# Rounded routing features, negations on ScalarE, a subtraction on GpSimd, and the spacing of zero writes in a three-stage kernel

## The chip, the core and the metric

The kernel runs on one core of one Trainium2 chip. The metric is the device time of one execution in microseconds; lower is better. TensorE (PE in the profile) multiplies, VectorE (DVE), ScalarE (ACT) and GpSimd (POOL) work on tiles, and SP issues most DMAs. Each engine takes its own instructions strictly in the order in which the build put them, and waits on semaphores for the others.

## What is computed

Three stages are chained. The input `x` is 4 batches of 3072 tokens of 256 numbers.

```python
# 1: spectral layer, per batch
X  = np.fft.rfft(x, axis=1)
Yr = X.real @ w_r - X.imag @ w_i + b_r
Yi = X.real @ w_i + X.imag @ w_r + b_i
Y  = sign(Y) * maximum(abs(Y) - 0.01, 0)       # real and imaginary part each
x  = np.fft.irfft(Y, n=3072, axis=1).reshape(12288, 256)
# 2: mixture of 8 experts, top 1, 384 places each, filled in token order
e  = argmax(x @ w_gate);  gate = softmax(...)[e]
h  = maximum(disp @ w1, 0);  y = h @ w2;  out[i] = gate[i] * y[e, place[i]]
# 3: dense layer
h  = x @ w_in;  out = (h * sigmoid(h)) @ w_out
```

Tokens that find no place give zero rows. With these inputs the experts are full early in batch 1, so the kernel works on batch 0 and a third of what follows, and a branch (never taken here) holds the rest.

## The kernel before

**Products.** Nearly all products run as three rounded passes (`mm3`, lines 208 to 210): each operand is split into a rounded high part and a rounded low part (`split`, lines 192 and 200), and high*high, low*high and high*low are summed in PSUM. Rounded tiles have the type FR (float32r), all others F32.

**Spectral stage.** `s1` makes the first half of the transform and stores it in DRAM (`a_d`). `kphase` then walks over 24 frequencies, two a step (k = 0, 2 to 22, 12 steps). `forward` makes the spectrum `xp` in PSUM (L418) and from it the tile `xk` with four parts: high (ACT, L432), low (DVE, L433), minus high (ACT, L434) and minus low (DVE, L435). `shrink` multiplies by the weights into `yp`, adds the bias (DVE, `y`, L456; the tile `y` has one buffer), clamps (DVE, L458) and subtracts the clamped part (DVE, L459), which gives `cl`. `back` (L465, `bp`) multiplies `cl` of three steps earlier by the inverse table; ACT copies `bp` to `bo` and after every second step issues its write to `b_d`. The steps of batch 0 are mixed with `s1` of batch 1 and with the rounding of `w_in`; those of batch 1 are mixed with `is2` of batch 0, which ends the inverse transform and computes the gate.

**Routing.** `route` counts places and builds `ft`, two features for each of 24 slots-by-expert columns (the token's number and its gate weight), and `pm`, a one-hot matrix for each group of 128 tokens. `tb = pm.T @ ft` (L723) is 24 F32 products for batch 0 and 8 for batch 1, each of which the chip runs as two passes. The sum goes to `table`, `slots` reads source rows and gate weights from it, `gather` fetches the rows with indirect DMAs on GpSimd (L978), DVE scales them (L982), PE transposes them (`gtp`, L990) and ACT and DVE split them into `xT`, which the first expert's product `hp` needs.

**Experts.** `experts` runs a first and a second phase per expert in the order first 0, 1, 2, second 0, 1, 2, first 3, 4, second 3, 4 and so on. Expert weights stream through four staging buffers (`st`, L966). Beside the first phases runs `third`, which reads `b_d` of batch 1 (`br`, L546) and makes the rows of its first third (`ps`, L549). Rows of the output that no token fills are written as zeros (`zero_out`, L217, 48 DMAs of 256 KB on SP). The finished rows go out by indirect DMAs on GpSimd (L1072).

A timeline planner in the build sets each engine's order from its own estimates, so that an edit also moves instructions that it doesn't name.

Of the kernel before, what the change touches and what calls it, by code (L numbers as in the profile page):

```python
# [9 lines left out]
F32 = mybir.dt.float32  # L10
FR = mybir.dt.float32r
I32 = mybir.dt.int32
ALU = mybir.AluOpType
AF = mybir.ActivationFunctionType
# [7 lines left out]
E, F, CAP = 8, 1024, 384  # L22
DFF = 2048
P = 128
# [4 lines left out]
NEAR = S + QB * TW  # L29
SC = CAP // P  # L30
NS = E * CAP
NF = 2
STEP = 4096
ROUND = 1.5 * 2.0 ** 30
MID = 0.5 * (P - 1)
# [107 lines left out]
def raw(t):  # L143
    return t.bitcast(F32)
# [18 lines left out]
class Kernel:  # L163
# [239 lines left out]
    def kphase(self, b, ads, ahead=False):  # L403

        nc, kp = self.nc, self.kp
        v = nc.vector
        a_d = ads[b]
        b_d = self.bds[b] = self.dr.tile([NK, P, D], F32, name=f"b_d{b}")
        KG = 4

        def fetch(k):
            ar = kp.tile([P, KG, D], F32, tag="ar", name="ar")
            self.fetched = nc.sync.dma_start(out=ar, in_=a_d[k:k + KG].rearrange("k p c -> p k c")).ins
            return ar

        def spectrum(xp, ar, kq, tb):

            return [nc.tensor.matmul(xp[:, c], ar[:, kq, c * P:(c + 1) * P], c2[:, tb], start=True, stop=True).ins for c in range(2)]  # L418

        def forward(k, ar):  # L420
            first = k == 0
            kq = k % KG
            xk = kp.tile([P, 2, 4, 192], FR, tag="xk", name="xk", bufs=3)
            xp = self.pk.tile([P, 4, P], F32, tag="xp", name="xp", bufs=self.xb)
            behind = self.gated[PACE[k // 2]] if b == 1 and k // 2 in PACE else None
            for j in range(2):
                for ins in spectrum(xp[:, 2 * j:2 * j + 2], ar, kq + j, k + j + 1):
                    if behind:
                        self.after(ins, behind)
            js = slice(2, 4) if first else slice(0, 4)  # L430
            up, mid, low = slice(64, 192), slice(128, 192), slice(0, 64)
            nc.scalar.copy(xk[:, 0, :, up], xp)  # L432
            v.tensor_tensor(xk[:, 1, :, up], xp, raw(xk[:, 0, :, up]), ALU.subtract)  # L433
            nc.scalar.activation(xk[:, 0, js, low], xp[:, js, 64:], AF.Copy, scale=-1.0)  # L434
            v.tensor_tensor(xk[:, 1, js, low], raw(xk[:, 0, js, mid]), xp[:, js, 64:], ALU.subtract)  # L435
            xo = None
            if first:
                xp = self.pk.tile([P, 4, P], F32, tag="xp", name="xp", bufs=self.xb)
                spectrum(xp, ar, 0, 0)
                xo = kp.tile([P, 2, 2, P], FR, name="xo", bufs=1)  # L440
                self.split("av", xo[:, 0], xo[:, 1], xp[:, :2])
            return xk, xo

        def shrink(k, xk, xo):
            yp = self.pk.tile([P, 2, D], F32, tag="yq" if k % 4 and (b != 1 or k > 12) else "yp", name="yp", bufs=1)
            for j in range(2):
                for jj in range(2):
                    for c in range(2):
                        if jj and xo is not None and not j:
                            l = [xo[:, h, c] for h in range(2)]  # L450
                        else:
                            l = [xk[:, h, 2 * j + c, 64 - 64 * jj:192 - 64 * jj] for h in range(2)]
                        self.mm3(yp[:, j], l[0], l[1], wri[:, jj, 0, c], wri[:, jj, 1, c], jj + c == 0, jj + c == 2)
            y = kp.tile([P, 2, D], F32, tag="y", name="y", bufs=1)
            bias = self.bias if xo is not None else self.bias[:, 1:2].to_broadcast([P, 2, D])
            v.tensor_tensor(y, yp, bias, ALU.add)  # L456
            cl = kp.tile([P, 2, D], F32, tag="cl", name="cl", bufs=3)
            v.tensor_scalar(cl, y, LAM, -LAM, ALU.min, ALU.max)  # L458
            self.shrunk = v.tensor_tensor(cl, y, cl, ALU.subtract).ins  # L459
            return cl  # L460

        def back(k, bo, cl):
            bp = self.pk.tile([P, 2, D], F32, tag="bp", name="bp", bufs=1)
            for j in range(2):
                self.backed = nc.tensor.matmul(bp[:, j], c3[:, k + j], cl[:, j], start=True, stop=True).ins  # L465
            self.hi("a", bo[:, k % KG:k % KG + 2], bp)
            if k % KG + 2 == KG:
                nc.scalar.dma_start(out=b_d[k + 2 - KG:k + 2].rearrange("k p c -> p k c"), in_=bo)

        x, y = {}, {}  # L470
        ars = [fetch(0), fetch(KG)] if ahead else []
        if ahead:
            yield
        c2, c3, wri = self.c2, self.c3, self.wri
        for k in range(0, NK + 6, 2):
            if k < NK:
                if k % KG == 0:
                    ar = ars.pop(0) if ars else fetch(k)
                x[k] = forward(k, ar)
            if 2 <= k < NK + 2:  # L480
                y[k - 2] = shrink(k - 2, *x.pop(k - 2))
            if k >= 6:
                if (k - 6) % KG == 0:
                    bo = kp.tile([P, KG, D], F32, tag="bo", name="bo")
                back(k - 6, bo, y.pop(k - 6))
            yield
# [168 lines left out]
    def route(self, b, qbs, res):  # L655

        nc, bp, ps, rt = self.nc, self.bp, self.ps, self.rt
        v = nc.vector
        oh, m2, sm = res[b]
        NB = len(qbs)  # L660
        NC = NB * GT
# [17 lines left out]
        nc.gpsimd.tensor_scalar(sm, sm, 1e-9, None, ALU.add)  # L679
        gt = bp.tile([P, NC, 1], F32, tag="gt", name="gt", bufs=1)  # L680
        v.reciprocal(gt, sm.rearrange("p b g o -> p (b g) o"))
        base = bp.tile([P, E, NB, 1], F32, tag="base", name="base", bufs=1)
        v.scalar_tensor_tensor(base[:, :, :, 0], bs[:, 0], -1.0, self.carry.to_broadcast([P, E, NB]), ALU.add, ALU.add)
        v.tensor_tensor(inc, base.to_broadcast([P, E, NB, GT]), oh, ALU.mult)
# [7 lines left out]
        r = bp.tile([P, NC, 1], F32, tag="r", name="r", bufs=1)  # L692
        v.scalar_tensor_tensor(r, blk, -ROUND, pos, ALU.add, ALU.subtract)
        sh = [P, NC, SC * E]
        ft = bp.tile([P, NC, NF, SC * E], F32, tag="ft", name="ft", bufs=1)
        mk = ft[:, :, 1]
        tok = rt[:, 2 * P + qbs[0] * GT:2 * P + qbs[0] * GT + NC].rearrange("p (c o) -> p c o", o=1)
        v.tensor_tensor(mk, blk.to_broadcast(sh), self.col.to_broadcast(sh), ALU.is_equal)
        v.tensor_tensor(ft[:, :, 0], mk, tok.to_broadcast(sh), ALU.mult)
        prev = v.tensor_tensor(mk, mk, gt.to_broadcast(sh), ALU.mult)  # L700
        tb = ps.tile([P, NF, SC * E], F32, tag="ps", name="tb")
        sh = [P, GT, P]
        for j in range(NB):
            pm = bp.tile(sh, F32, tag="xt", name="pm", bufs=self.sb)
            how = "v" if b else PMS[j]
            if how == "a":
                for t in range(GT):
                    nc.scalar.activation(pm[:, t], self.iota, AF.Abs, scale=-1.0, bias=r[:, j * GT + t])
                nc.scalar.activation(pm, pm, AF.Relu, scale=-1.0, bias=1.0)
            elif how == "v":  # L710
                here = v.tensor_tensor(pm, self.iota.rearrange("p (o m) -> p o m", o=1).to_broadcast(sh),
                                       r[:, j * GT:(j + 1) * GT].to_broadcast(sh), ALU.is_equal)
                self.after(here.ins, prev.ins)
                self.made = here.ins
            else:
                for t in range(GT):
                    e = v if how == "s" else nc.gpsimd
                    here = e.tensor_scalar(pm[:, t], self.iota, r[:, j * GT + t], None, ALU.is_equal)
                    if how == "s":
                        self.after(here.ins, prev.ins)  # L720
                        self.made = here.ins
            for t in range(GT):
                nc.tensor.matmul(tb, pm[:, t], ft[:, j * GT + t], start=(j + t == 0), stop=(j * GT + t == NC - 1))  # L723
# [35 lines left out]
    def slots(self, pool, s0, s1, sel, tag):  # L759

        v = self.nc.vector
# [14 lines left out]
        v.tensor_scalar(a, ent[:, :, 0:SC], -1.0, 0.0, ALU.add, ALU.max)  # L776
        v.tensor_copy(src, a)
        gw = pool.tile(w, F32, name=f"gw{tag}", bufs=1)
        v.tensor_copy(gw, ent[:, :, SC:2 * SC])
        b = pool.tile(w, F32, name=f"slb{tag}", bufs=1)  # L780
        dst = pool.tile(w, I32, name=f"dst{tag}", bufs=1)
        v.tensor_scalar(b, ent[:, :, 0:SC], 0.5, BIG, ALU.is_lt, ALU.mult)
# [88 lines left out]
    def experts(self, again=False):  # L871
# [44 lines left out]
        n = 0  # L916
        for at, ph in enumerate(order):
# [11 lines left out]
            for m, _ in enumerate(part):  # L929
                n += 1  # L930
                while due is not None and due <= n:
                    due = next(side, None)
                if n in AHEAD or (ph == E and m % 2 == 0):
                    next(fw, None)
                if ph >= E:
                    for _ in range(2 if ph == E else n % 2):
                        self.zero_out()
                if m == last - 2 and after < E:
                    xs[after] = self.turn(xg.pop(after))
# [179 lines left out]
```

## Time and profile before

| | |
|---|---|
| median of 3 runs | 649.71 us (649.0 to 649.79) |
| profiled execution: time, span | 650.9 us, 649.1 us |
| PE busy | 618.7 us (95%) |
| DVE, ACT, POOL busy | 320.3 us (49%), 305.8 us (47%), 75.5 us (12%) |
| granted TensorE clock, mean | 0.975 of full speed |

Busy time of PE is modelled, and a busy PE may be a slow one: at half of the granted clock a pass takes twice as long and still counts as busy. So the table by stretches is read with its column of the granted clock (PEclk), and the pitch of passes (start to start) is read from the timeline.

### The profile page before, as it was taken

How to read it: one execution, taken by the hardware profiler on the slowest of the kernel's cores; microseconds unless marked ns; L12 is line 12 of the kernel's file. 1: busy time of each engine (PE TensorE's matmuls, PEld its weight loads, DVE VectorE, ACT ScalarE, POOL GpSimd, SP SyncE). 2: the span in 40 equal slices, each digit the busy share in tenths (PEclk: the TensorE clock that was granted, in tenths of full speed). 3: DMA queues.
4: the chain of work that ended last, by engine and by line, in shares of the span. 5: the costliest groups of instructions: out<-in, count | busy, mean ns of one | idle time of the engine just before them, and what ended most of it. 6: DMA issues, size and time to landing. Idle time of an engine off the chain costs nothing. (4 is left out here: it accounts for less than half of the span.)

```text
span 649.1 us, 10932 instructions
## 1 busy us (share of the span) xinstructions
PE 618.7 (95%) x4108; PEld 567.7 (87%) x4108; DVE 320.3 (49%) x655; ACT 305.8 (47%) x624; POOL 75.5 (12%) x86
## 2 busy tenths in 40 slices
PE   7689999999998999999999999999999999999993
PEld 3367889767997679999999999999999999999993
DVE  3349986455966467886222246522236632223330
ACT  4434543343433445466544445545445554544450
POOL 1002220000023001062101032000121000101001
PEclk7899999999977999999999999999999999999998
DMA  8996945983337776599700025300004300000000
GB/s 251 294 264 210 303 153 174 200 258 96 130 123 219 215 203 218 167 310 330 246 1 26 1 71 149 110 5 10 16 21 127 119 13 2 25 1 25 1 2 29
DMA packets 64085, 83.03 MB, mean 128 GB/s; under 512 B 5588, under 2 KB 53688, under 8 KB 64024
## 3 DMA queue, kind: packets, MB, share of 16 engines
q1 hardware_dynamic: 52056, 66.52, 33.9%
q10 hardware_dynamic: 9664, 9.44, 4.9%
q0 software_dynamic: 2304, 6.29, 3.0%
q8 instruction: 34, 0.56, 0.3%
q14 instruction: 27, 0.22, 0.1%
HBM read 49.73 MB, written 32.51 MB: 127 GB/s over the span
## 5 line engine op out<-in xcount | busy, mean ns | idle before, releaser
L200 DVE TENSOR_TENSOR gl<-sg,gh 128x384 fp32r<-128x384 f32 x118 | 67.1, 574 | 160.6 <-ACT gh L192 154.7
L1042 ACT ACTIVATE sg<-h 128x384 f32<-128x384 f32 x128 | 62.4, 491 | 108.6 <-PE h L210 103.8
L209 PE MATMUL o<-wo,gl 128*128 128x256 f32 x354 | 93.2, 282 | 0.5 <-DVE gl L200 0.5
L210 PE MATMUL o<-wo,gh 128*128 128x256 f32 x354 | 93.1, 282 | 0.0
L208 PE MATMUL h<-yT,wi 128*128 128x384 f32 x256 | 86.3, 337 | 0.4 <-ACT yT L192 0.4
L209 PE MATMUL h<-yT,wi 128*128 128x384 f32 x256 | 86.1, 336 | 0.0
L210 PE MATMUL h<-yT,wi 128*128 128x384 f32 x256 | 85.7, 337 | 0.0
L208 PE MATMUL o<-wo,gh 128*128 128x256 f32 x354 | 74.6, 282 | 0.0
L209 PEld LDWEIGHTS o<-wo,gl 128*128 128x128 f32 x354 | 67.1, 190 | 0.9 <-DVE gl L200 0.7
L210 PEld LDWEIGHTS o<-wo,gh 128*128 128x128 f32 x354 | 67.2, 190 | 0.0
L192 ACT CAST gh<-sg 128x384 fp32r<-128x384 f32 x118 | 59.9, 514 | 6.9 <-PE o L210 4.0
L208 PEld LDWEIGHTS o<-wo,gh 128*128 128x128 f32 x354 | 60.3, 189 | 0.0
L208 PE MATMUL yp<-wri,xk 128*128 128x256 f32 x188 | 56.3, 299 | 0.1
L209 PE MATMUL yp<-wri,xk 128*128 128x256 f32 x188 | 55.0, 293 | 0.3 <-DVE xk L435 0.3
L210 PE MATMUL yp<-wri,xk 128*128 128x256 f32 x188 | 54.0, 287 | 0.0
L200 DVE TENSOR_TENSOR w<-st,w 128x512 fp32r<-128x512 f32 x64 | 44.4, 696 | 17.3 <-ACT w L192 17.2
L192 ACT CAST w<-st 128x512 fp32r<-128x512 f32 x64 | 39.3, 620 | 28.3 <-PE hp L210 14.8
L1008 ACT ACTIVATE hh<-hp 128x384 fp32r<-128x384 f32 x64 | 31.3, 491 | 41.6 <-PE hp L210 18.6
L208 PEld LDWEIGHTS h<-yT,wi 128*128 128x128 f32 x256 | 48.2, 188 | 0.7 <-ACT yT L192 0.7
L1009 DVE SCALAR_TENSOR_TENSOR hl<-hp,hh 128x384 fp32r<-128x384 f32 x64 | 35.0, 553 | 27.3 <-ACT hh L1008 24.9
L209 PEld LDWEIGHTS h<-yT,wi 128*128 128x128 f32 x256 | 48.1, 188 | 0.0
L210 PEld LDWEIGHTS h<-yT,wi 128*128 128x128 f32 x256 | 48.1, 188 | 0.0
(213 smaller groups left out, 1214.4 us busy)
## 6 DMA issues: line engine op xcount, KB each, us to landing
st<-in_moe_w SPq DMA_DIRECT2D x64, 256.0 KB
out<-zt SPq DMA_DIRECT2D x48, 256.0 KB
a_d<-ao SPq DMA_DIRECT2D x16, 384.0 KB
ar<-a_d SPq DMA_DIRECT2D x12, 512.0 KB
b_d<-bo ACTq DMA_DIRECT2D x12, 512.0 KB
xt<-in_x SPq DMA_DIRECT2D x15, 384.0 KB
nt<-in_moe_w_in SPq DMA_DIRECT2D x8, 512.0 KB
nt<-in_moe_w_out SPq DMA_DIRECT2D x16, 256.0 KB
```

Of the source, the lines that this page charges most:

```text
L192: self.nc.scalar.copy(dst, src)
L200: return e.tensor_tensor(dst, src, raw(hi), ALU.subtract).ins
L208: first = nc.tensor.matmul(out, lh, rh, start=start, stop=False)
L209: nc.tensor.matmul(out, ll, rh, start=False, stop=False)
L210: return first.ins, nc.tensor.matmul(out, lh, rl, start=False, stop=stop).ins
L1008: nc.scalar.activation(hh, hp, AF.Relu)
L1009: self.evicted = nc.vector.scalar_tensor_tensor(hl, hp, 0.0, raw(hh), ALU.max, ALU.subtract).ins
L1042: nc.scalar.activation(sg, hp, AF.Silu)
```

## The change

Four edits. (1) The negated low part is made by ScalarE from the finished low part, not by VectorE from PSUM. (2) The routing product runs on rounded operands: the gate weight is split into a rounded high and low part, so there are three features and not two, `mk` gets a tile of its own, and `slots` adds the two parts. (3) The last subtraction of `shrink` runs on GpSimd in batch 1. (4) While the second phase of expert 0 runs, each of its steps issues one zero write and not two.

```diff
-NF = 2
+NF = 3
@@ forward
-            v.tensor_tensor(xk[:, 1, js, low], raw(xk[:, 0, js, mid]), xp[:, js, 64:], ALU.subtract)
+            nc.scalar.activation(xk[:, 1, js, low], raw(xk[:, 1, js, mid]), AF.Copy, scale=-1.0)
@@ shrink
-            self.shrunk = v.tensor_tensor(cl, y, cl, ALU.subtract).ins
+            if b == 1:
+                nc.gpsimd.tensor_tensor(cl, y, cl, ALU.subtract)
+            else:
+                self.shrunk = v.tensor_tensor(cl, y, cl, ALU.subtract).ins
@@ route
+        gh = bp.tile([P, NC, 1], FR, tag="gh", name="gh", bufs=1)
+        gl = bp.tile([P, NC, 1], FR, tag="gl", name="gl", bufs=1)
+        self.split("vv", gh, gl, gt)
...
-        ft = bp.tile([P, NC, NF, SC * E], F32, tag="ft", name="ft", bufs=1)
-        mk = ft[:, :, 1]
+        ft = bp.tile([P, NC, NF, SC * E], FR, tag="ft", name="ft", bufs=1)
+        mk = bp.tile(sh, F32, tag="mk", name="mk", bufs=1)
...
-        prev = v.tensor_tensor(mk, mk, gt.to_broadcast(sh), ALU.mult)
+        v.tensor_tensor(ft[:, :, 1], mk, raw(gh).to_broadcast(sh), ALU.mult)
+        prev = v.tensor_tensor(ft[:, :, 2], mk, raw(gl).to_broadcast(sh), ALU.mult)
...
-            pm = bp.tile(sh, F32, tag="xt", name="pm", bufs=self.sb)
+            pm = bp.tile(sh, FR, tag="xt", name="pm", bufs=self.sb)
@@ slots
-        v.tensor_copy(gw, ent[:, :, SC:2 * SC])
+        v.tensor_tensor(gw, ent[:, :, SC:2 * SC], ent[:, :, 2 * SC:], ALU.add)
@@ experts
-                    for _ in range(2 if ph == E else n % 2):
+                    for _ in range(1 if ph == E else n % 2):
```

The build moves instructions too. GpSimd's order around the first gathers, before; `wi` and `wo` are low parts of the dense layer's weights, `sm`, `ex`, `pl` and `big` small steps of routing, `xg` the gathers of experts 0 to 2, three each:

```order
L200 TENSOR_TENSOR wi<-na,wi 128x512 x8
L679 TENSOR_SCALAR sm<-sm 128x24
L675 TENSOR_SCALAR ex<-m_1063 128x24
L749 TENSOR_TENSOR pl<-sel,num 128x64
L755 TENSOR_TENSOR big<-sel,carry 128x24
L978 DMA xg<-attn_69,srcs 128x256 x9
L200 TENSOR_TENSOR wo<-na,wo 128x512 x2
```

and now:

```order
L460 TENSOR_TENSOR cl<-y,cl 128x512 x5
L678 TENSOR_SCALAR ex<-m_1063 128x24
L682 TENSOR_SCALAR sm<-sm 128x24
L460 TENSOR_TENSOR cl<-y,cl 128x512 x4
L756 TENSOR_TENSOR pl<-sel,num 128x64
L762 TENSOR_TENSOR big<-sel,carry 128x24
L460 TENSOR_TENSOR cl<-y,cl 128x512
L985 DMA xg<-attn_69,srcs 128x256 x6
L460 TENSOR_TENSOR cl<-y,cl 128x512
L985 DMA xg<-attn_69,srcs 128x256 x3
L460 TENSOR_TENSOR cl<-y,cl 128x512
```

The last three of the twelve subtractions (k = 18, 20 and 22) now stand before, between and behind the gathers.

PE's order where the first expert begins, before:

```order
L465 MATMUL bp<-cl,c_242 128x256 x2
L990 MATMUL gtp<-ident,xg 128x128 x4
L465 MATMUL bp<-cl,c_242 128x256 x2
L990 MATMUL gtp<-ident,xg 128x128 x2
L208 MATMUL hp<-xT,w_2109 128x384
L209 MATMUL hp<-xT,w_2109 128x384
L465 MATMUL bp<-cl,c_242 128x256 x2
L210 MATMUL hp<-xT,w_2109 128x384
```

and now:

```order
L468 MATMUL bp<-cl,c_242 128x256 x2
L997 MATMUL gtp<-ident,xg 128x128 x6
L208 MATMUL hp<-xT,w_2115 128x384
L209 MATMUL hp<-xT,w_2115 128x384
L468 MATMUL bp<-cl,c_242 128x256 x2
L210 MATMUL hp<-xT,w_2115 128x384
```

The `bp` of k = 20, which stood between the transposes, now comes behind the first two passes of `hp`, and the one of k = 22 sixteen passes of `hp` later. The routing product of batch 0 moved the other way, ahead of more of batch 1: 52 `yp` passes and five `bp` follow it where 41 and four did. The first `ps` of `third` stands 41 rounded passes behind the transposes where it stood 47.

## Rows read from the trace of the kernel before

**Rows 1.** Table by stretches: start:end, length, busy us (instructions) per engine, PEclk, DMA share, GB/s.
```profile
181.60:186.40 4.80, 4.80 (x45) 4.80 (x45) 3.67 (x13) 0.52 (x2) 0.51 (x2) 1.00 0.33 113
186.40:193.30 6.90, 6.90 (x30) 6.54 (x30) 3.14 (x13) 1.24 (x2) 2.52 (x3) 0.51 0.55 171
193.30:200.10 6.80, 4.67 (x35) 4.25 (x34) 4.96 (x11) 3.33 (x6) 4.10 (x4) 1.00 0.77 238
200.10:206.90 6.80, 6.17 (x19) 5.02 (x18) 3.79 (x9) 1.95 (x5) 2.99 (x3) 0.50 0.73 225
...
300.00:630.00 330.00, 327.85 (x2201) 325.99 (x2200) 122.65 (x224) 168.16 (x351) 31.65 (x31) 1.00 0.18 56
```
**Rows 2.** Timeline of PE: start, us, line, tiles, shape, count, idle before and its releaser.
```profile
181.78 6.07 PE L723 MATMUL tb<-ft,pm 128*128 128x48 f32 x48
...
193.31 0.28 PE L209 MATMUL yp<-wri,xk 128*128 128x256 f32 x1
193.43 0.28 PE L210 MATMUL yp<-wri,xk 128*128 128x256 f32 x1
...
196.06 1.03 PE L465 MATMUL bp<-cl,c 128*128 128x256 f32 x4
196.92 0.60 PE L990 MATMUL gtp<-ident,xg 128*128 128x128 f32 x4
...
201.13 0.63 PE L990 MATMUL gtp<-ident,xg 128*128 128x128 f32 x2
202.39 0.69 PE L208 MATMUL hp<-xT,w 128*128 128x384 f32 x1 [0.63 <-ACT xT L192]
...
203.19 1.91 PE L465 MATMUL bp<-cl,c 128*128 128x256 f32 x4
...
207.74 0.33 PE L209 MATMUL hp<-xT,w 128*128 128x384 f32 x1
207.92 0.33 PE L210 MATMUL hp<-xT,w 128*128 128x384 f32 x1
...
215.04 1.05 PE L549 MATMUL ps<-br,c 96*32 96x512 f32 x4 [0.78 <-DMA br<-b_d]
```
**Rows 3.** Groups by line and shape: busy us, mean ns; idle before and releasers.
```profile
L459 DVE TENSOR_TENSOR cl<-y,cl 128x512 f32<-128x512 f32 x24 | 16.5, 688 | 0.5
L435 DVE TENSOR_TENSOR xk<-xk,xp 128x256 fp32r<-128x256 f32 x22 | 9.2, 418 | 6.3 <-ACT xk L434 6.3
L434 ACT ACTIVATE xk<-xp 128x256 fp32r<-128x256 f32 x22 | 8.4, 382 | 14.7 <-DVE xk L433 14.7
L200 POOL TENSOR_TENSOR wo<-na,wo 128x512 fp32r<-128x512 f32 x8 | 11.1, 1388 | 73.4 <-ACT wo L192 51.2 <-PE hp L210 22.1
```
**Rows 4.** Timeline of PE's weight loads in batch 0, where one waits.
```profile
72.03 0.19 PEld L209 LDWEIGHTS yp<-wri,xk 128*128 128x128 f32 x1 [0.46 <-DVE xk L435]
```
**Rows 5.** Timeline of DVE, with GpSimd busy (first, third) and idle (second).
```profile
72.61 1.34 DVE L458 TENSOR_SCALAR cl<-y 128x512 f32<-128x512 f32 x1
...
77.17 0.43 DVE L458 TENSOR_SCALAR cl<-y 128x512 f32<-128x512 f32 x1
...
271.54 1.01 DVE L730 TENSOR_TENSOR table<-table,ob 128x24 f32<-128x24 f32 x1
```
**Rows 6.** Timeline of GpSimd: first and sixth gather.
```profile
190.17 1.23 POOL L978 DMA_INDIRECT xg<-attn,srcs  x1 [4.86 <-ACT w L192]
...
197.32 0.99 POOL L978 DMA_INDIRECT xg<-attn,srcs  x1 [0.30 <-issue]
```
**Rows 7.** DMA issues by line: the gathers, median us from issue to landing.
```profile
xg<-attn,srcs POOLq DMA_INDIRECT x9, 2.9
```
**Rows 8.** Timeline of the queues of ACT and SP: last write of b_d, first reads.
```profile
205.76 0.37 ACTq L468 DMA_DIRECT2D b_d<-bo  x1
...
209.94 0.84 SPq L546 DMA_DIRECT2D br<-b_d  x2
```
**Rows 9.** Timeline of GpSimd: first scatter of finished rows.
```profile
314.02 1.03 POOL L1072 DMA_INDIRECT out<-oo,dsts  x1 [9.93 <-DMA out<-zt]
```

More of the change, by code (lines that the diff above doesn't have):

```diff
@@ L708, in route @@
                     nc.scalar.activation(pm[:, t], self.iota, AF.Abs, scale=-1.0, bias=r[:, j * GT + t])
-                nc.scalar.activation(pm, pm, AF.Relu, scale=-1.0, bias=1.0)
+                nc.scalar.activation(pm, raw(pm), AF.Relu, scale=-1.0, bias=1.0)
             elif how == "v":
```

## The prediction

> **What bounds the kernel now.** I read the table by stretches first. From 300 to 630 us PE is busy 327.85 of 330 us at full clock [rows 1]: that half of the run is PE's own work, which the change doesn't touch. What it can move is PE's work, or PE's lost time, before that. The largest loss stands between 186 and 215 us. From 186.4 to 193.3 and from 200.1 to 206.9 the granted clock is about 0.5 (1.2 GHz, not 2.4), and from 193.3 to 200.1 PE is busy only 4.67 of 6.80 us [rows 1]. Before the first fall PE was not idle: it ran the 48 passes of `tb`, 48 columns each, without a gap [rows 1, 2]. Before the second it waited for the copy of `bp` and for the gathered rows.
>
> How large is the loss? From 186.4 to the first `ps` at 215.04 are 28.6 us [rows 1, 2]. The work in it at full clock: five `tb` passes left (0.6), 41 `yp` passes at 0.12 (193.31 to 193.43) = 4.9, four `bp` at 0.86 (196.06 to 196.92) = 3.4, transposes 0.7, and 47 passes of `hp` and `y` at 0.18 (207.74 to 207.92) = 8.5; together 18.1. So 10.5 us are lost there.
>
> **Part 1, rounded routing product.** The 48 passes take 6.07 us, the last five at half clock; in the full-clock stretch 45 instructions take 4.80 us [rows 1, 2], so a pass costs some 0.11. There are 64 with batch 1: 64 x 0.11 = 7.0 us. Now there are 32, of 72 columns. No row shows a rounded pass of so few columns. Upper bound: 0.22, as the F32 pair costs now. Lower bound: half of the pass, 0.055, if rounded weights load twice as fast. I take 0.11, the nearest row (same weights, few columns), and it lies under the 0.12 of a rounded pass of 256 columns. Gain 7.0 - 3.5 = **3.5 us** (bounds 0 and 5.3), all on PE and so on the path. VectorE pays for it in `route`: one more product of 576 columns and two tiny splits, about 1.1 us per call in batch 0, covered below.
>
> **Part 2, negation on ScalarE.** 24 operations of 418 ns leave DVE and 24 of about 382 ns go to ACT [rows 3], 10.0 and 9.2 us. ACT is busy 47%, and the new operation follows L434, which already waits for the low part (14.7 us of idle before it [rows 3]); so nothing new is waited for. Its cover is PE's `yp` pass; without it, 0.4 us a step. In batch 0 PE's weight loads wait now and then for DVE, as 0.46 us for L435 [rows 4]; I count some 0.7 us of that as won (bounds 0 and 1.5, three such places).
>
> **Part 3, subtraction on GpSimd.** 12 x 688 ns = 8.3 us leave DVE, and 12 x 1.39 us = 16.7 us go to GpSimd [rows 3]. Two new waits come with it. `y` has one buffer, so the next bias addition waits until GpSimd has read the last; with steps of some 4.6 us of PE work that is covered. And DVE isn't free meanwhile: a clamp that starts under a GpSimd subtraction takes 1.34 us instead of 0.43, and an addition of 24 columns 1.01 [rows 5]. So of the 0.69 a step that DVE wins, up to 0.9 may go again where `route` follows.
> The Trainium skill says (SBUF — State Buffer, "Who interferes with whom") that a VectorE operation with two SBUF inputs and a GpSimd operation that reads SBUF exclude one another for a whole instruction. By that rule alone the trade would be a loss for DVE: 12 blocks of 1.3 us against 8.3 won, some 7 us of DVE time. The rows agree that it blocks; operations that read PSUM are outside the rule.
>
> Where it costs is the stretch after routing. Call T the end of `tb` for batch 0, now 187.6. In the changed order PE has six `yp` (0.7), three `xp` (0.7) and one `bp` (0.9) less to do before it, and 24 passes of `tb` less (2.7, and 0.5 at half clock): T = 187.6 - 5.5, about 182. DVE must have `pm` ready by then; the 4.4 us that four steps win there pay for the 1.1 of part 1 and some 3 of blocking, so it's close, 0 to 1.5 us late.
> After T, now: gathers start at T + 2.5 (190.17), six take 8.1 us (190.17 to 198.31) [rows 6], the third lands 2.9 after its issue [rows 7]. In the changed order the bias and clamp of k = 18 (1.1) stand before the source rows on DVE, and their subtraction (1.3) before the gathers on GpSimd: start T + 4 to T + 5. Third row landed and scaled: T + 10 to T + 11. PE is there earlier, at T + 8.8 (52 x 0.12 + 3 x 0.86), and waits 1.4 to 2.4. `hp` starts 1.9 after that, at T + 12 to 13 (before: transposes, then 1.3 from 201.13 to 202.39 [rows 2]). The subtraction of k = 20 stands behind six gathers: T + 13.5 to 14.5, so `bp` waits about 1.2. That of k = 22 stands behind three more gathers (3.9) and itself takes 1.3: T + 19 to 20; PE, with 16 `hp` passes (2.9) meanwhile, waits 1.5 to 2. The write of `b_d` follows 1.6 later, at 203 to 204 against 205.76 now [rows 8]. Now SP issues the read 4.2 us after that (209.94), behind weight loads, and `ps` runs 9.3 after. In the changed order the weight loads ahead of it are done; 6.3 us (two flights of about 2.9 [rows 7] and the issues) give `ps` at 209.5 to 210.5, and PE, with 23 passes (4.1) from `bp`, waits about 3.
> Sum of waits: 1.9 + 1.0 + 1.2 + 1.8 + 3.0 = 8.9. The thin stretch from T + 9 to T + 14 very likely brings one stretch of half clock: it costs 0.8 where PE waits anyway, up to 3.4 (half of 6.8 [rows 1]) where it has work; I take 2. So the loss is 10.9, against 10.5 now: **0.4 us worse**. Bounds: 6 (no fall, gathers early) and 17.
>
> **Part 4, zeros.** The first scatter waits 9.93 us for zero writes [rows 9], on GpSimd and far from PE: nothing on the path. Spread later, at most nine zeros pass between weight loads, which are fetched over an expert ahead. I take 0, bounds -0.5 and +0.7.
>
> **Sum.** -3.5 - 0.7 + 0.4 + 0 = -3.8 on the profiled execution's 650.9 (span 649.1 and 1.8 around it). That execution lies 1.2 above the median; the differences are taken over to the median: 649.7 - 3.8, about **645.9 us**.
>
> **The clock, by the page.** The first fall came behind `tb` passes that left no gap [rows 1, 2]; with half as many, I expect it gone. The Trainium skill (TensorE: Matmul & The Clock Gate, "What's actually happening") has the throttle return when PE is idle; by that rule the fall is not the work of `tb`, and stays. Then the stretch behind `tb` runs at half clock again: 6.9 us of work and loss of 3.4, of which PE would have waited 2 for the gathers anyway: 1.4 more, 647.3. The trace speaks against it; I give it 0.08, inside the forecast's own range.
>
> **Rivals.** (a) The waits stay small: gathers start at T + 2.5 as now, GpSimd's queue never holds `bp`, no clock falls. Loss 6 instead of 10.9: 645.9 - 4.9 = 641.0. For it: the planner spread the subtractions between the gathers. Against: strict order on GpSimd. Chance 0.20.
> (b) Given back: T late by 1.5, and both the thin stretch and the wait for `br` bring half clock (3.4 more): 645.9 + 3.4 to 4.5, about 649.8. Also that the rounded pass costs 0.22, so that part 1 does nothing: 649.4. Chance 0.20.
> (c) Slower: GpSimd's queue takes the place of the clock. If the three subtractions take 2 us each and block the source rows on DVE again, `bp` of k = 22 ends some 3 us later, and `br`, `third` and the clock follow: loss 17, 652.0. It decides where that `bp` ends: behind 206 us the change loses. Chance 0.11.
>
> **How the numbers follow.** Forecast 0.49 (643 to 648), (a) 0.20, (b) 0.20, (c) 0.11. The range 640.5 to 650.0 leaves out (c) and the outer ends of (a) and (b), some 0.2 in all. About 0.2% (1.3 us) is what a measurement of this kernel can tell from no change: faster 0.69, same 0.20, slower 0.11.
>
> **What would show it.** Right: 32 `tb` passes some 0.11 apart; full clock directly behind them; T near 182; idle on PE before `bp` with GpSimd as its cause; `ps` near 210. Wrong: `tb` passes at 0.22; PE waiting for `pm` before them; a `bp` of k = 22 behind 206; waits for expert weights near 400 us, where the later zeros pass.

## The result, and the profile after

| | before | changed |
|---|---|---|
| median (4 runs each) | 649.36 us | 659.02 us (656.31 to 660.76) |
| profiled execution: span | 649.1 us | 657.3 us |
| PE, DVE, ACT, POOL busy | 618.7, 320.3, 305.8, 75.5 us | 618.8, 311.0, 313.3, 93.9 us |

The changed kernel takes 1.0131 of the time before, 95% interval 1.0099 to 1.0164: **slower by 8.5 us**, where I forecast 3.8 us faster. Measured again beside the experiments it was 1.0119 (1.0059 to 1.0179). The forecast was wrong in sign and the range did not hold the time.

Single executions of one kernel lie up to some 5 us either side of its median, so verdicts below go by ratios with intervals, and a profile is read for where time goes, not for how much a kernel takes.

First the stretch in which the prediction saw the cost, 186 to 226 us. Columns: start:end, length, busy us (instructions) of PE, PE's weight loads, DVE, ACT and POOL, granted clock, DMA share, GB/s. The kernel before:

```profile
186.00:226.00 40.00, 36.40 (x178) 29.60 (x177) 22.02 (x50) 13.89 (x27) 9.60 (x9) 0.83 0.69 207
```

The changed kernel, the same stretch:

```profile
186.00:226.00 40.00, 30.05 (x146) 24.96 (x146) 19.54 (x45) 12.39 (x24) 14.51 (x15) 0.83 0.65 191
```

The mean granted clock is the same, 0.83, and PE is idle for 9.95 us, not 3.6. What PE waited for in that stretch (engine, tile, line, releaser: us in total, times, longest), before:

```profile
PE bp L465 <- ACT bo L192: 2.1, 1, 2.1
PE ps L549 <- DMA br<-b_d: 0.8, 1, 0.8
PE hp L208 <- ACT xT L192: 0.6, 1, 0.6
```

and in the changed kernel:

```profile
PE ps L552 <- DMA br<-b_d: 3.4, 2, 2.2
PE bp L468 <- ACT w L192: 2.6, 1, 2.6
PE gtp L997 <- DVE xg L989: 2.0, 1, 2.0
PE y L208 <- ACT hh L1015: 1.6, 1, 1.6
PE hp L208 <- ACT xT L192: 0.4, 1, 0.4
```

The timeline of PE shows where they stand (start, us, line, tiles, shape, count, idle before and its releaser):

```profile
182.79 0.98 PE L730 MATMUL tb<-ft,pm 128*128 128x72 f32 x8
...
183.81 1.87 PE L730 MATMUL tb<-ft,pm 128*128 128x72 f32 x16
...
196.26 1.73 PE L468 MATMUL bp<-cl,c 128*128 128x256 f32 x4 [2.56 <-ACT w L192]
...
201.12 0.69 PE L997 MATMUL gtp<-ident,xg 128*128 128x128 f32 x2 [2.04 <-DVE xg L989]
202.16 0.69 PE L208 MATMUL hp<-xT,w 128*128 128x384 f32 x1 [0.35 <-ACT xT L192]
202.96 1.91 PE L468 MATMUL bp<-cl,c 128*128 128x256 f32 x4
...
208.46 1.02 PE L468 MATMUL bp<-cl,c 128*128 128x256 f32 x4
211.09 0.44 PE L208 MATMUL y<-hh,w 128*128 128x384 f32 x1 [1.61 <-ACT hh L1015]
...
217.56 1.05 PE L552 MATMUL ps<-br,c 96*32 96x512 f32 x4 [2.21 <-DMA br<-b_d]
219.78 1.27 PE L552 MATMUL ps<-br,c 96*32 96x512 f32 x4 [1.17 <-DMA br<-b_d]
```

The passes of the routing product are as fast as forecast: 24 of 72 columns, (1.87 - 0.27) / 15 = 0.107 us apart. They are done at T = 185.6, where the kernel before had 187.6 and the forecast about 182. Then the `bp` of k = 22 comes at 208.46, where it stood at 203.19 [rows 2]; the first product `y` of the expert waits for ACT, and the first two `ps` wait for `br`. What made that `bp` late shows on GpSimd and VectorE. GpSimd:

```profile
198.96 1.27 POOL L460 TENSOR_TENSOR cl<-y,cl 128x512 f32<-128x512 f32 x1
202.08 1.02 POOL L985 DMA_INDIRECT xg<-attn,srcs  x1 [1.84 <-DVE xg L989]
203.41 1.00 POOL L985 DMA_INDIRECT xg<-attn,srcs  x1 [0.30 <-issue]
204.71 1.00 POOL L985 DMA_INDIRECT xg<-attn,srcs  x1 [0.30 <-issue]
205.74 1.28 POOL L460 TENSOR_TENSOR cl<-y,cl 128x512 f32<-128x512 f32 x1
```

VectorE in the same stretch: a low part of weights under the subtraction of k = 20, then the bias addition and the clamp of k = 22:

```profile
198.67 2.13 DVE L200 TENSOR_TENSOR w<-st,w 128x512 fp32r<-128x512 f32 x1 [0.34 <-ACT w L192]
...
203.08 0.68 DVE L456 TENSOR_TENSOR y<-yp,bias 128x512 f32<-128x512 f32 x1
...
204.42 0.41 DVE L458 TENSOR_SCALAR cl<-y 128x512 f32<-128x512 f32 x1
```

The subtraction of k = 20 stands behind six gathers and ends at 200.23. Until then it holds the one buffer of `y`, so the build puts the bias addition of k = 22 late on VectorE: 203.08, where the kernel before had it at 198.23:

```profile
198.23 0.69 DVE L456 TENSOR_TENSOR y<-yp,bias 128x512 f32<-128x512 f32 x1 [1.83 <-PE bp L465]
```

Its clamp ends at 204.83, and its subtraction stands behind three more gathers: 205.74 to 207.02. From there the `bp` could have run, but in PE's order it stands behind all passes of the first `hp`, and that takes 1.4 us more. ACT then copies `bp` and goes on to `hh` behind it, and the write of `b_d` is issued; SP issues the read 3.4 us later (before: 205.76 and 209.94 [rows 8]). ACT and its queue:

```profile
209.52 0.59 ACT L192 COPY bo<-bp 128x512 f32<-128x512 f32 x1 [1.28 <-PE bp L468]
210.13 0.37 ACTq L471 DMA_DIRECT2D b_d<-bo  x1
210.54 0.87 ACT L1015 ACTIVATE hh<-hp 128x384 fp32r<-128x384 f32 x2 [0.44 <-ACT bo L192]
```

SP's queue:

```profile
213.49 1.03 SPq L549 DMA_DIRECT2D br<-b_d  x2
```

**How much it is.** From the start of the last `tb` pass of batch 0 to the first of batch 1 it took 81.2 us before and 91.6 in both profiled executions of the changed kernel (the second is that of the repeat at the end of the experiments). The `tb` of batch 1, before and now:

```profile
268.66 1.88 PE L723 MATMUL tb<-ft,pm 128*128 128x48 f32 x16
```

```profile
277.00 0.98 PE L730 MATMUL tb<-ft,pm 128*128 128x72 f32 x8
```

Counted in the trace, 11 `yp`, 4 `bp` and 12 `hp` or `y` passes more lie in that stretch now (11 x 0.12 + 4 x 0.215 + 12 x 0.173 = 4.3 us at full clock). So 10.4 - 4.3 = **6.1 us are lost** there, in each of the two. Against that stand 3.2 us won in the 24 passes of batch 0 and 0.9 in the 8 of batch 1. The rest of the 8.2 us between the two spans, moved work taken off in the same way: 3.3 ahead of `tb` (0.9 in the second execution) and 2.9 behind the `tb` of batch 1 (3.0), of which a new wait near 300 us is the largest piece (below).

Of the 3.3 us, 2.0 lie ahead of the first `yp` pass of batch 1 (107.46 before, 109.44 now) and so ahead of every subtraction that moved; in the second execution that part is -0.3, so it is scatter. The other part, from that pass to `tb`, is 1.3 us (1.2), and it comes again: 1.2 to 1.5 us in all seven profiles of kernels with the first eight subtractions on GpSimd, 0 to 0.4 in the ten other profiles of the experiments.

### The profile page after: what moved, and what is told of

The parts are those of the page before. It is cut to its first block, busy times and chain, and to the rows that moved or that the text cites. A ratio compares the mean times of both kernels' runs of the same rounds, so it can differ in the third digit from the quotient of the medians.

```text
span 657.3 us, 10893 instructions
## 1 busy us (share of the span) xinstructions
PE 618.8 (94%) x4076; PEld 564.6 (86%) x4076; DVE 311.0 (47%) x625; ACT 313.3 (48%) x648; POOL 93.9 (14%) x98
## 5 line engine op out<-in xcount | busy, mean ns | idle before, releaser
L200 DVE TENSOR_TENSOR w<-st,w 128x512 fp32r<-128x512 f32 x64 | 46.3, 730 | 26.2 <-ACT w L192 26.2
L208 PE MATMUL yp<-wri,xk 128*128 128x256 f32 x188 | 55.6, 296 | 0.9 <-ACT xk L432 0.9
L192 ACT CAST w<-st 128x512 fp32r<-128x512 f32 x64 | 39.2, 620 | 33.6 <-PE hp L210 14.8
L209 PE MATMUL yp<-wri,xk 128*128 128x256 f32 x188 | 54.1, 288 | 0.5 <-DVE xk L433 0.4
L210 PE MATMUL yp<-wri,xk 128*128 128x256 f32 x188 | 53.6, 285 | 0.0
```

Of the source, the lines that this page charges most:

```text
L192: self.nc.scalar.copy(dst, src)
L200: return e.tensor_tensor(dst, src, raw(hi), ALU.subtract).ins
L208: first = nc.tensor.matmul(out, lh, rh, start=start, stop=False)
L209: nc.tensor.matmul(out, ll, rh, start=False, stop=False)
L210: return first.ins, nc.tensor.matmul(out, lh, rl, start=False, stop=stop).ins
```

## Experiments

Each kernel runs the whole computation. The number is the time over that of the kernel before on the same chip.

| kernel | ratio, 95% interval | idle + clock, 186 to 226 us |
|---|---|---|
| changed | 1.0131 (1.0099 to 1.0164) | 9.9 + 6.8 |
| edit 1 alone | 1.0030 (0.9999 to 1.0062) | 6.2 + 3.6 |
| edit 2 alone | 0.9967 (0.9935 to 0.9999) | 4.7 + 5.2 |
| edit 3 alone | 1.0095 (1.0064 to 1.0125) | 6.5 + 8.4 |
| edit 4 alone | 0.9979 (0.9945 to 1.0014) | 2.8 + 3.6 |
| edit 3, k below 16 | 1.0042 (1.0006 to 1.0079) | 4.9 + 5.2 |
| edit 3, k = 16 and 18 | 0.9992 (0.9959 to 1.0024) | 3.8 + 5.2 |
| edit 3, k = 20 | 1.0031 (0.9996 to 1.0066) | 8.3 + 3.6 |
| edit 3, k = 22 | 1.0026 (0.9998 to 1.0055) | 8.2 + 1.6 |
| edit 3, k = 20 and 22 | 1.0101 (1.0054 to 1.0148) | 9.9 + 5.2 |
| edit 3, k = 16 to 22 | 1.0093 (1.0062 to 1.0123) | 9.0 + 3.6 |
| edits 1, 2, 4 | 1.0002 (0.9969 to 1.0034) | 5.8 + 1.6 |
| changed, k = 20 and 22 on VectorE | 1.0002 (0.9973 to 1.0031) | 4.9 + 5.2 |
| changed, k = 22 on VectorE | 1.0113 (1.0070 to 1.0155) | 9.4 + 5.2 |
| changed, `y` twice | 1.0103 (1.0039 to 1.0168) | 10.3 + 5.2 |
| edits 2, 4 | 0.9961 (0.9936 to 0.9986) | 3.8 + 5.2 |

The last column is worked out from the profile's row for 186 to 226 us: 40 less PE's busy time, and 40 x (1 - PEclk), which is what half clock takes. Idle time at half clock counts in both, so their sum is an upper end. Each is of a single execution. The kernel before has 3.6 + 6.8.

**The four edits, one at a time.** Each is the hunk of the diff ahead of the prediction, put on the kernel before.

> The kernel before with the first edit alone: minus low is made by ScalarE from the finished low part. In the changed kernel batch 0 was already 1.5 us late at 78 us and 3.3 us late at 163 us, with PE waiting for ScalarE's xk (0.92) and bo (0.36). Theory A (the negation costs: ScalarE is late for xk and bo): 3 us slower than the kernel before, about 652.5, with the same stalls between 60 and 165 us. Rival B (those stalls came with GpSimd's or the routing edit through the build's order, the negation is free): within 1 us of the kernel before, 648.5 to 650.

> The kernel before with the second edit alone: the routing product on rounded operands, 32 passes of 72 columns for 64 of 48. Theory A (the passes' 3.5 us are won and nothing else moves): 645.5 to 646.5, 32 passes some 0.11 us apart, and the first read of b_d in third no later than before (215). Rival B (what follows the routing is bound by GpSimd's gathers, the copies of bp and the fall of the clock, so that the gain is given back behind it): 648.5 to 650, third's first pass near 215.

> The kernel before with the third edit alone: the subtraction of shrink on GpSimd in batch 1. Theory A (GpSimd's queue is the cause of the slower time: subtractions between the gathers delay the bp of k = 20 and 22, and third with them): 4 to 8 us slower, 653.5 to 657.5, bp of k = 22 behind 206 us, third's first pass behind 217. Rival B (the delay there came from the order of ScalarE, with the weight casts ahead of bo, which the other edits bring): within 1.5 us of the kernel before.

> The kernel before with the fourth edit alone: one zero write a step and not two while the second phase of expert 0 runs. Theory A (harmless): 649 to 650, within 0.7 us of the kernel before. Rival B (the zeros that come later stand between weight reads on SP, and GpSimd's gathers of batch 1's rows then stand ahead of the low part of w_out, as in the changed kernel at 300 us, where PE lost 3.7 us): 3 to 4 us slower, with PE waiting near 300 us for ScalarE's sg.

Measured: 652.03, 647.14, 657.04 and 648.12 us beside 649.49. Edit 3 alone is slower by 6 us: its theory A held (its `bp` of k = 22 at 209.10, the first `ps` at 218.02), and edits 1, 2 and 4 don't have such a loss. Edit 2 wins about 2 of the 4.1 us that its passes save, between its two theories. `third` begins no later (212.89), but PE, early now, waits 2.5 us for gathered rows and 1.5 for `hl`. Edit 1 wins nothing; it may cost 2 us, and the interval touches no change. In its one profile PE waits 1.6 us for `bo` and `xk` between 40 and 182 us, where the kernel before waits 0.3, which are the stalls of its theory A. Edit 4 is no slower; its gain can't be told from none.

**Which of the twelve subtractions.** On the kernel before:

```diff
-            if b == 1:
+            if b == 1 and k < 16:
```

and its complement, `k >= 16`.

> The kernel before with the third edit for eight of its twelve steps (k below 16): these subtractions run on GpSimd, the last four stay on VectorE, so that none stands among the gathers. All twelve made it 6 us slower. Theory A (GpSimd's queue between and behind the gathers is the cause): the loss is gone, 648.5 to 651, the bp of k = 22 before 205 us and third's first pass near 215. Rival B (GpSimd's longer subtraction and its blocking of VectorE cost in the steps ahead of the routing product too): 652 to 654, and the routing product of batch 0 begins 1 us late or more (183).

> The kernel before with the third edit for the last four steps alone (k = 16 to 22), the complement of the run on the first eight. Theory A (the queue among the gathers): nearly the whole 6 us, 654 to 657, with bp of k = 22 near 208 and third's first pass near 218. Rival B (it is the eight earlier steps): 649 to 652.

Measured: 652.16 and 655.41 beside 649.51. The last four cost as much as all twelve, the time of their theory A, though in the profile, of the fastest execution, that `bp` (205.70) and the first `ps` (215.33) come earlier than it said. The first eight cost something too: their time lies in the range of rival B, with an interval from 0.4 to 5 us. The 1.2 us ahead of `tb` (above) are a part of it. `tb` begins at 183.96, as B said, but 2.1 us of that lateness stand there before batch 1 begins. Where the rest is lost was not found.

```diff
-            if b == 1:
+            if b == 1 and k == 22:
```

and `k in (16, 18)`, both on the kernel before.

> The kernel before with a single one of the twelve subtractions on GpSimd, the last (k = 22), which stands behind all nine gathers there. Theory A (the last subtraction behind the gathers delays bp of k = 22, with it the write of b_d, the read by third and ScalarE's hh): 652 to 656, bp of k = 22 near 206 or later, PE waiting for hh and over 2 us for br. Rival B (what costs is that the subtractions of k = 16 and 18 hold back the source rows and the start of the gathers): within 1.5 us of the kernel before.

> The kernel before with two subtractions on GpSimd, k = 16 and 18, both ahead of the gathers; k = 20 and 22 stay on VectorE. Theory A (only what stands behind gathers costs): 648.5 to 651. Rival B (the source rows come late): 652.5 to 655.5, with the first gather 1.5 us or more behind that of the kernel before (190.2).

Measured: 650.75 and 649.1 beside 649.65. The two ahead of the gathers cost nothing, and the first gather is not late (189.67): rival B, the late source rows, falls. The last one alone costs less than theory A said (its time is within the 1.5 us of B), though the waits that A named are there: 1.6 us for `hh` and 3.1 for `br`. The subtraction began at 199.33 and the `bp` at 200.67, since VectorE's bias addition and clamp of k = 22 were not held up by k = 20.

**In the changed kernel.** Without edit 3; then with k = 20 and 22 back on VectorE; then with a second buffer for `y` (and for line 330, which shares it).

```diff
-            if b == 1:
+            if b == 1 and k <= 18:
```

```diff
-            y = kp.tile([P, 2, D], F32, tag="y", name="y", bufs=1)
+            y = kp.tile([P, 2, D], F32, tag="y", name="y", bufs=2)
```

> The changed kernel with the third edit undone: edits one, two and four. The single edits measured 1.003, 0.997 and 0.998 of the kernel before. Theory A (edits add up, and the third alone makes the change slower): 647 to 650, and no stall near 300 us. Rival B (the stall of 3.7 us near 300 us, where ScalarE waits for a low part of w_out that stands behind six gathers on GpSimd, comes of edits one, two and four together; the build has the same order of GpSimd there): 651 to 654, with that stall.

> The changed kernel with the subtractions of k = 20 and 22 back on VectorE; the other ten stay on GpSimd. Without the third edit it measured 649.4, and eight early subtractions alone cost some 2.7 us. Theory A (the two behind gathers carry the rest): 650 to 653, bp of k = 22 before 205, no stall near 300 us. Rival B (the ten others carry it too): 655 to 659.

> The changed kernel with a second buffer for y, so that the bias addition of k = 22 needn't wait until GpSimd has subtracted k = 20. With it the build puts the subtractions of k = 20 and 22 together ahead of the last three gathers; no other work is added. Theory A (the place in GpSimd's queue and the wait for y's buffer make the last subtraction late): bp of k = 22 at 204 to 206 and not 208.5, 652 to 655. Rival B (it is GpSimd's blocking of VectorE and the fall of the clock, wherever the subtraction stands): 657 to 660.

Measured: 649.44 beside 649.51, 649.92 and 655.11 beside 649.65. **With two of twelve subtractions back on VectorE the loss is gone**, as with all twelve; each of these two ratios is known to some 2 us. With the two on VectorE, PE waited in 186 to 226 us for:

```profile
PE bp L468 <- ACT bo L192: 2.2, 1, 2.2
PE gtp L997 <- DVE xg L989: 1.5, 2, 0.8
PE y L210 <- DVE hl L1016: 0.6, 1, 0.6
PE hp L208 <- ACT xT L192: 0.6, 1, 0.6
```

The waits for `hh` and `br` are gone: the bias addition of k = 22 comes behind a subtraction on VectorE and in front of one, its `bp` stands among the first passes of `hp` (201.44), and the write of `b_d` goes out at 204.00. The timeline of VectorE in that kernel:

```profile
194.68 0.69 DVE L462 TENSOR_TENSOR cl<-y,cl 128x512 f32<-128x512 f32 x1
...
196.19 0.68 DVE L456 TENSOR_TENSOR y<-yp,bias 128x512 f32<-128x512 f32 x1
...
199.47 0.68 DVE L462 TENSOR_TENSOR cl<-y,cl 128x512 f32<-128x512 f32 x1
```

and of ACT's queue:

```profile
204.00 0.37 ACTq L471 DMA_DIRECT2D b_d<-bo  x1
```

The stretch between the two `tb` takes 82.2 us there, with 0.1 us more work than before: 0.9 lost and not 6.1.

The second buffer of `y` freed the bias addition (196.56), as wanted, and put both subtractions ahead of the last three gathers, yet gave back little, if anything: 655.11 is at the upper end of theory A, and the interval, from 2.5 to 11 us above the kernel before, holds the range of B too. Both subtractions now ran beside VectorE's work, and gathered rows were scaled late. VectorE in that kernel:

```profile
197.16 1.81 DVE L989 TENSOR_SCALAR xg<-xg,gws 128x256 f32<-128x256 f32 x1
...
200.68 1.36 DVE L989 TENSOR_SCALAR xg<-xg,gws 128x256 f32<-128x256 f32 x1
```

and GpSimd:

```profile
200.07 1.82 POOL L460 TENSOR_TENSOR cl<-y,cl 128x512 f32<-128x512 f32 x1 [1.27 <-DVE cl L458]
```

The subtraction of k = 22 ended at 201.89, but PE's order had its `bp` only at 206.14, right ahead of `y`, and 1.6 us for `hh` and 2.8 for `br` were waited for as before:

```profile
206.14 1.02 PE L468 MATMUL bp<-cl,c 128*128 128x256 f32 x4
...
208.77 0.44 PE L208 MATMUL y<-hh,w 128*128 128x384 f32 x1 [1.61 <-ACT hh L1015]
```

The stretch between the two `tb` lost 5.1 us there, against 6.1. So the place that the build gave that `bp` is part of the loss, beside the queue. No kernel was run in which the subtractions move and PE's order stays, so how the loss divides between the two is not shown.

**One or the pair.**

```diff
-            if b == 1:
+            if b == 1 and k == 20:
```

and `k >= 20` on the kernel before, `k <= 20` on the changed kernel, and the changed kernel itself once more.

> The kernel before with the subtraction of k = 20 alone on GpSimd, behind six gathers; k = 22 stays on VectorE. Theory A (the pair costs together): within 2 us of the kernel before, as k = 22 alone (1.7). Rival B (k = 20 alone carries it, by holding y's one buffer): 653 to 656, and the bias addition of k = 22 on VectorE behind 200.

> The kernel before with k = 20 and 22 on GpSimd, no other subtraction. Theory A (the pair costs what all twelve cost): 654 to 657. Rival B (the pair costs the sum of the two alone, and the rest comes of the earlier ones): 651 to 653.

> The changed kernel with the subtraction of k = 22 alone back on VectorE; k = 20 stays on GpSimd behind six gathers. Theory A (the pair): 650 to 652.5, no wait of PE for hh near 209. Rival B (k = 20 carries it): 655 to 658.

> The changed kernel itself, on the same chip as the three others. By its first runs 657 to 660. If the stall near 300 us (3.7 us) belongs to its order it is in this profile too; if it hung on when the gathered rows and the weights landed in one execution, it may be missing, with a time near 655.

Measured: 652.74, 655.51, 658.95 and 657.98 beside 650.47. On the kernel before, the two alone add up to 1.0057 and the pair measured 1.0101; the intervals are too wide to call the difference shown. On the changed kernel theory A falls: with k = 22 back on VectorE it is as slow as ever. GpSimd's subtraction of k = 20 is enough there: the bias addition of k = 22 comes behind it, and `hh` and `br` are waited for 1.6 and 3.1 us. The reverse, k = 22 without k = 20 on GpSimd, was not run on the changed kernel. GpSimd of that kernel:

```profile
204.17 1.27 POOL L460 TENSOR_TENSOR cl<-y,cl 128x512 f32<-128x512 f32 x1
```

and VectorE, bias addition and subtraction of k = 22:

```profile
207.12 0.68 DVE L456 TENSOR_TENSOR y<-yp,bias 128x512 f32<-128x512 f32 x1
...
208.91 0.69 DVE L462 TENSOR_TENSOR cl<-y,cl 128x512 f32<-128x512 f32 x1
```

The repeat of the changed kernel has the wait near 300 us again (2.24 us, at 301.64). In its first profile PE waits for ACT, ACT for a low part of `w_out` on GpSimd, and that stands behind six gathers of an expert's rows. PE of the changed kernel there:

```profile
303.23 0.44 PE L208 MATMUL h<-yT,wi 128*128 128x384 f32 x1 [2.21 <-ACT sg L1049]
```

ACT:

```profile
302.14 0.66 ACT L843 ACTIVATE na<-nt 128x512 f32<-128x512 f32 x1 [6.39 <-POOL wo L200]
```

GpSimd, the last of the six and two low parts:

```profile
299.80 1.00 POOL L985 DMA_INDIRECT xg<-attn,srct  x1 [0.30 <-issue]
300.82 2.50 POOL L200 TENSOR_TENSOR wo<-na,wo 128x512 fp32r<-128x512 f32 x2
```

The kernel with k = 20 and 22 on VectorE loses as much a little earlier (2.19 us at 289.77, for `gl`) and is level with the kernel before; so this wait is not what decides between the two.

**A faster version.** Edits 2 and 4 alone:

> The kernel before with edits two and four alone, which were the two that made it no slower. If they add up (0.997 and 0.998): 645 to 647.5, faster than both kernels. Rival (both gains come of the same stretch between 190 and 220 us, where PE waits for gathers and b_d anyway): no better than the better of the two, 647 to 648.5. The tables of GpSimd's order have one low part of w_out ahead of the six gathers here, as the kernel before, so no stall is expected near 300 us.

Measured: 646.2 beside 649.51, 0.9961 (0.9936 to 0.9986). It is the fastest of all, 2.5 us below the kernel before, and little better than edit 2 alone: the expectation's two cases can't be told apart.

## Why the prediction was wrong

**The sign was lost in part 3**, which I put at 0.4 us worse and which lost 6.1. Its stretch was followed on the right engines and in the right order, but nearly each step came later than worked out. T is 185.6 in the first profile of the changed kernel and 183.2 in the second, for about 182 and 0 to 1.5 late; the blocking of VectorE that this allowed for is the 1.3 and 1.2 us above, the rest is scatter. Times behind T:

| | forecast | first | second | before |
|---|---|---|---|---|
| first gather | 4 to 5 | 5.0 | 5.5 | 2.6 |
| `hp` | 12 to 13 | 16.6 | 15.7 | 14.8 |
| `bp` k = 20 | 13.5 to 14.5 | 17.4 | 16.5 | 12.1 |
| `bp` k = 22 | 19 to 20 | 22.9 | 21.4 | 15.6 |
| first `ps` | 27.5 to 28.5 | 32.0 | 30.6 | 27.4 |

Three terms failed. First, the gathers: I took 8.1 us for six, as before; they took 8.4, and in the second execution 9.2 (188.66 to 197.84), and the rows were scaled by a VectorE that GpSimd blocked. Second, `y`: I named its one buffer and held it covered "with steps of some 4.6 us of PE work". It is covered as long as GpSimd subtracts at once; behind six gathers it is not, and k = 20 alone then costs the changed kernel all of it. That the buffer by itself is the cause is not shown, since a second one gave back little. Third, the waits moved: I forecast 1.2 and 1.8 us before the two `bp` and got none, since the build had put work in front of them; in their place came 1.6 for `hh`, because ACT copies `bp` first, and 2.6 before an earlier `bp`, for ACT's weight casts (2.1 before).

In sum the waits were nearly right: 8.9 forecast, 9.9 and 9.4 measured. **The half clock was mis-sized.** I gave it 2 us. The row for 186 to 226 us has 0.83, as before: 40 x 0.17 = 6.8 us, and some 5.6 without half of the 2.4 us in which PE was idle anyway. 9.9 + 5.6 = 15.5 us of loss against 10.5 before, 5.0 more, where the stretch measured 6.1. The bound of 17 held it; I took 10.9, with the fall behind `tb` gone. It did go (full clock from 182 to 195 us), but the clock fell at 196.6, behind PE's wait of 2.6 us, and at 220.5, behind the waits for `br`, and stayed at half for 10.2 and 3.4 us. The changed kernel's row for the stretch behind `tb`, where the kernel before had 0.74:

```profile
182.00:195.00 13.00, 11.70 (x94) 11.28 (x92) 8.85 (x26) 3.32 (x8) 6.59 (x8) 1.00 0.45 139
```

So the rival by which the fall stays did not come. But my own reason, that the 48 passes of `tb` make the clock fall, is not borne out either. Ten of the profiled kernels keep these passes, and in none does the trace show PE idle in the 10 us ahead of their end. In four the clock fell around it (the kernel before, edit 3 alone, edit 4 alone, k = 16 and 18). In six it stayed full (edit 1 alone; edit 3 for k below 16, k = 16 to 22, k = 20, k = 22, k = 20 and 22). With k = 20, for example, `tb` ended at 186.3 us, and its row is:

```profile
181.00:193.00 12.00, 12.00 (x99) 11.59 (x97) 8.03 (x27) 3.15 (x6) 3.83 (x6) 1.00 0.57 173
```

So the full clock behind `tb` may have been luck, and what makes it fall there stays open. The later falls of the changed kernel, each behind an idle PE, agree with what the clock page of the Trainium skill (TensorE: Matmul & The Clock Gate, "What's actually happening") says of idle time.

**Part 1** was right: 0.107 us a pass, 4.1 us saved, against 3.5; 0.5 of it because the last passes before ran at half clock. But alone it brings 2: PE gets earlier to rows and copies that it must wait for. **Part 2** came out the other way: 0.7 us gained was forecast, 1.9 us lost measured alone, and 0.9961 against 1.0002 without and with it beside edits 2 and 4; each interval just touches nothing, so the sign is likely and not certain. Its cover was ACT's idle time; where in the kernel it costs was not settled. **Part 4** was right: no new wait near 400 us.

**What the sum left out.** From 300 us on I had read PE's work as untouched. Behind the `tb` of batch 1 the changed kernel loses 2.9 us (3.0), of which 2.2 is the new wait at 303 us. So the 12 us between the forecast of -3.8 and the 8.2 between the spans are 5.7 in part 3's stretch, 2.9 behind it, and 4.0 ahead of `tb` (the 0.7 of part 2, 1.3 under the early subtractions, 2.0 of scatter), less 0.6 that part 1 won more.

Two readings were wrong without consequence. The work taken from ahead of `tb` is 12 `yp` passes and one `bp` (1.44 + 0.86 us) and no `xp`; that it sums to the 2.3 of my list was luck. And before the second fall PE of the kernel before waited for ACT alone, not for gathered rows.

**Rivals.** Rival (c) named GpSimd's queue and got 0.11; the clock fell as well. Its price of 2 us a subtraction was too high (1.27 to 1.40 in the first profile), and its point of decision, that the `bp` of k = 22 ends behind 206 us, was wrong: in the second execution it ended at 205.75, and the stretch lost 6 us all the same. It had to be measured from T, which was 4.4 us earlier there: from T the chain of k = 22 ran 21.4 us, not 15.6.

**DVE and GpSimd.** The rule that I quoted from the Trainium skill (SBUF — State Buffer, "Who interferes with whom") is borne out again: 2.13 us for a low part that takes 0.68 with GpSimd idle. The 12 subtractions took 1.29 us each, 15.5 in all, against 16.7 forecast.

## What to carry to other kernels

An operation moved to an engine that also issues gathers is priced by what stands ahead of it in that queue and by the places that the build then gives to what depends on it, not by its own duration; and where its input has one buffer, the next step's first operation waits for the same queue. Leave the last steps, on which a write and a read back depend, where they were. The steps far from the gathers are not free either: ten of them gained nothing that could be measured. When PE is made faster ahead of such a chain, measure the chain from PE's new time: part of what PE gains it waits for, and a wait of PE can bring a stretch of half clock (here 5.6 us on 9.9 us of waits).

## What the runs showed of the hardware that I had not expected

A rounded pass of 72 columns follows the next after 0.107 us, half of the F32 pair of 48 columns (0.22). Behind the same 48 passes of 48 columns, without a gap on PE, the granted clock fell to half in four profiles and stayed full in six. Issuing an indirect DMA on GpSimd for the first experts' rows took 0.99 to 1.50 us, later once 3.20 (290.67 us, changed kernel); in the second execution of the changed kernel four of nine took 1.3 or more, and a queue of six was 1.1 us longer for it. And an operation of VectorE lost up to 2.1 us beside GpSimd: the scaling of gathered rows (0.34) took 2.44 us at 301 us in the changed kernel, under two low parts of `w_out`.
